# Fused block-sparse attention and gated projection on one Trainium2 core: where GpSimd makes a row tile's fourth low part, and where the gathers of the values stand

## The chip, the cores and the metric

The kernel runs on one core of one Trainium2 chip. The core has a matrix engine (TensorE, PE in the profile; PEld is its weight load), a vector engine (VectorE, DVE), a scalar engine (ScalarE, ACT), GpSimd (POOL), and SyncE (SP), which here only issues DMAs. Each engine works through its own instructions in order, and the engines wait for each other by semaphores. The metric is the device time of one execution in microseconds, as a median over several executions.

## The reference, cut to what matters

Attention over 4 batches, 8 heads, 768 positions and a head width of 64, in blocks of 32 positions. A query block sees itself, its two neighbours, the first and the last block, and three sampled blocks; the first and last query blocks see everything. Then a gated projection over d = 512:

```python
scores = where(mask, q @ k.T / 8, -1e9);  x = softmax(scores) @ v        # (B, S, 512)
gate   = sigmoid(sum_k conv_w[k] * shift(x, 4 - k))                      # causal, 5 taps, per channel
out    = (gate * (x @ w_val)) @ w_out
```

All of it is float32 in and out.

## The kernel before, in words

**Attention.** The work of a batch is 11 pairs of query blocks and one global pair (the first and last blocks), which counts as two units; 52 units in all. The main loop (lines 704 to 768) is a software pipeline over steps n. A step computes the scores of unit n on TensorE (`sc`, for global units `s`; `scores`, line 374), the transposes of unit n-1 (`pt`, line 423) and the values of unit n-2 (`av`, line 434). VectorE takes the maxima (`mx`), ScalarE the exponentials (`pe`) and the copies of the transposes out of PSUM (`ptr`). `finish` (line 476) turns the result around on TensorE (`xp`) and ScalarE copies it to `xT`. The scores of a global unit need a PSUM buffer in batches 2 and 3 that `xp` held, so TensorE waits there until ScalarE has made the copy `xT`.

**Keys and values.** GpSimd copies neighbour key blocks of a pair into `kg` two steps ahead (`copy_keys`, line 299). The rows of `v` that a pair needs are gathered by two indirect DMAs that GpSimd issues (`vb`, in `load_values`, line 317). `next_values` (line 742) issues them in step n for a pair that is read by the values of step n+3. The buffer that they fill is the one that the values of step n free, so each pair of gathers waits for the `av` matmuls of its own step.

**Projection.** 384 rows of a batch make a row tile; there are eight, numbered 1 to 8 here. Float32 operands are split into a high and a low part that TensorE multiplies in three passes. ScalarE makes the high parts (`xh`, `yh`), GpSimd the low ones (`xl`, `yl`) by a subtraction that needs the high part. VectorE builds the gates (`th`, a chain of multiply-adds with both tensor inputs in SBUF) and the product of gate and value projection (`y`, in `evict`).

`project` (line 551) is a generator, and each call of `advance` runs one piece of it. Pieces 1 to 4 are the value projections `vp` of the four column groups f = 0 to 3. Pieces 5 to 10 are the halves of three output groups `op`. In the kernel before, low part f is made by `second(f)`:

```python
for f in range(CH):            # piece f + 1
    if f > 1: second(f - 2)
    if f: evict(f - 1)
    ...                        # the 12 matmuls of vp[f], then yield
second(CH - 2)                 # piece 5: the third low part
evict(CH - 1)                  #          and the fourth y and yh
```

Piece 5 then issues the first half of the first `op`. Piece 6 begins with `second(CH - 1)`, the fourth low part, and then issues the second half of that `op`, whose last three matmuls are on group 3: twice its high part, and last its low part. `y` has two buffers, so `evict(f)` waits for `second(f - 2)`.

**The order around the change.** In each step the loop passes over the halves of `transposes`; in half i it calls `fill(FILLS[2n+i])`, which runs that many pieces of the projection, then `prepare`, which runs pieces of the gates (`th`) and of the split (`xh`, `xl`) of a later row tile, then `next_values`. `next_values` also stands ahead of the halves (line 746), and there it issues what is to be issued, unless `before_last_low` says that piece 6 falls into the first half of this step; then the gathers come behind that half. FILLS and STEPS are strings of digits written by hand.

By these strings piece 5 and piece 6 fall so: row tile 1, step 23 second half and step 24 first half; tile 2, step 29 second and step 30 first; tile 3, step 35 first and step 35 second; tile 4, step 40 second and step 41 first; tile 5, step 45 third pass (a global unit has three) and step 46 first; tile 6, step 51 second and step 52 first; tiles 7 and 8 behind the loop. Gathers are issued in steps 23, 24, 29, 30, 35, 40 and 41; in steps 45, 46, 51 and 52 none is left to issue. Step 29 begins with its scores at 172.2 us, step 30 at 179.0 us, step 35 at 215.9 us, and step 36 at 224.6 us.

Of the kernel before, what the change touches and what calls it, by code (L numbers as in the profile page):

```python
# [22 lines left out]
CH = 4  # L23
# [9 lines left out]
LAG_T, LAG_V = 1, 2  # L33
# [13 lines left out]
FILLS = (  # L47
    "11111210010222221221011022"
    "22111000222222111202211111"
    "02021011111110020111111002"  # L50
    "11211111221001111120020111"
    "1200"
)
# [11 lines left out]
def attention_moe(ctx, tc, qb, kb, v, ve, sampled, w_val, conv_w, w_out, ident_in, slot_in, out):  # L65
# [97 lines left out]
    def indices(b):  # L163

        row = const.tile([128, NB], F32, tag=f"row{b % 2}", name="row")
        dve.tensor_scalar_add(row, base, float(b * S - B * S))
        dve.tensor_tensor(out=row, in0=row, in1=valid, op=ALU.mult)
        dve.tensor_scalar_add(idx[:, b, :], row, float(B * S))
# [100 lines left out]
    def block_numbers(pr, eng):  # L269

        mine = [n for n in range(2 * NR) if COPIED[pr.bt.b].get(n, SP) == eng]
        if not mine:
            return
        first = NR * PAIRS[pr.p][0] + mine[0]
        _, regs = nc.values_load_multi_w_load_instructions(
            sm[0:1, first : first + len(mine)], engines=[eng], min_val=0, max_val=NB - 1,
            skip_runtime_bounds_check_because="block numbers are drawn from [0, 24)",
        )
        for n, reg in zip(mine, regs):
            yield 5 + 4 * (n // NR) + n % NR, reg  # L280
# [270 lines left out]
    def project(m):  # L551

        yh = const.tile([128, CH, TS], F32R, tag="yh", name="yh")
        yl = const.tile([128, CH, TS], F32R, tag="yl", name="yl")
        ys, vps = {}, {}

        def evict(f):
            y = ys[f] = two.tile([128, TS], F32, tag="y", name="y")[:, 0 : m.n]
            dve.scalar_tensor_tensor(
                out=y, in0=m.th[:, f, 0 : m.n], scalar=1.0, in1=vps[f][:, 0 : m.n], op0=ALU.add, op1=ALU.mult  # L560
            )
            act.copy(yh[:, f, 0 : m.n], y)

        def second(f):
            pool.tensor_tensor(
                out=yl[:, f, 0 : m.n], in0=ys[f], in1=yh[:, f, 0 : m.n].bitcast(F32), op=ALU.subtract
            )

        for f in range(CH):
            if f > 1:  # L570
                second(f - 2)
            if f:
                evict(f - 1)
            vps[f] = ps_moe.tile([128, 512], F32, tag="mo", name="vp")
            n = 0
            for wn, xn in ((0, m.xh), (1, m.xh), (0, m.xl)):
                for c in range(CH):
                    matmul(
                        vps[f][:, 0 : m.n], wv[wn][:, c, f * 128 : (f + 1) * 128], xn[:, c, 0 : m.n],
                        start=n == 0, stop=n == 11,  # L580
                    )
                    n += 1
            if f == CH - 1:
                unread.discard(id(m))
            yield
        second(CH - 2)
        evict(CH - 1)
        gating.discard(id(m))

        def leave(r, op):  # L590
            ot = two.tile([128, DM], F32, tag="ot", name="ot")
            row = m.t + r * 128
            if m.bt.b == B - 1 and row + 128 == S:
                act.activation(ot[:, 0:256], op[:, 0:256], AF.Copy, scale=0.5)
                dve.tensor_scalar(out=ot[:, 256:512], in0=op[:, 256:512], scalar1=0.5, scalar2=None, op0=ALU.mult)
                act.dma_start(out[m.bt.b, row : row + 128, 0:256], ot[:, 0:256])
                sp.dma_start(out[m.bt.b, row : row + 128, 256:512], ot[:, 256:512])
                return
            act.activation(ot, op, AF.Copy, scale=0.5)
            stores.append((out[m.bt.b, m.t + r * 128 : m.t + r * 128 + 128, :], ot))  # L600

        before = None
        for r in range(m.n // 128):
            op = ps_moe.tile([128, 512], F32, tag="mo", name="op")
            n = 0
            terms = [(f, yh, w) for f in range(CH - 1) for w in wo] + [(f, yl, wo[0]) for f in range(CH - 1)]
            for f, yn, w in terms + [(CH - 1, yh, wo[0]), (CH - 1, yh, wo[1]), (CH - 1, yl, wo[0])]:
                matmul(op, yn[:, f, r * 128 : (r + 1) * 128], w[:, f, :], start=n == 0, stop=n == 11)
                n += 1
                if n == 6:  # L610
                    if before is not None:
                        leave(*before)
                    yield
                    if r == 0:
                        second(CH - 1)
            before = r, op
            yield
        leave(*before)

    to_gate, to_split, to_project = [], [], []  # L620
    unread, gating, stores = set(), set(), []

    def store():
        while stores:
            sp.dma_start(*stores.pop(0))
# [27 lines left out]
    def may_project():  # L653
        return "all" in decoded and to_project and step[0] > max(to_project[0][0].ready)
# [4 lines left out]
                to_project[0][0].groups += 1  # L659
                advance(to_project)  # L660

    def before_last_low(times):

        return may_project() and to_project[0][0].groups <= CH + 1 < to_project[0][0].groups + times

    def prepare(steps):
        for _ in range(steps):
# [15 lines left out]
    def freed(k):  # L683

        return units[min(k, N - 1)].pr.seq if k >= 0 else -1

    def more(which, upto, load):
        if at[which] < len(pairs) and pairs[at[which]].seq <= upto:
            load(pairs[at[which]])
            at[which] += 1  # L690
            return True

    def until(which, n, do):
        while at[which] < min(len(pairs), pairs.index(units[min(n, N - 1)].pr) + 1):
            do(pairs[at[which]])
            at[which] += 1
# [7 lines left out]
    for n in range(N + LAG_V):  # L704
        step[0] = n

        def more_keys():
            return more("keys", freed(n - 1) + RING, load_keys)

        def more_values():  # L710
            return more("values", freed(n - LAG_V - 1) + VRING, load_values)

        if n == 0:
            more_keys()
            numbers_first = {eng: list(block_numbers(pairs[0], eng)) for eng in (POOL, ACT)}
            until("scaled", 0, scale)
            indices(0)
            until("copied", 0, copy_keys)
            more_keys()
            until("copied", 1, copy_keys)  # L720
            more_values()
        else:
            while more_keys() or more_values():
                more_values()
        until("scaled", n + (SCALE_AHEAD if n else 1), scale)
        store()
        k = len(staged)
        if k < 2 * CH and n >= WEIGHTS_AT[k] and (k < 4 or k - 4 in decoded):
            next(weights)

        if n < N:
            scores(units[n])
        if n == 0:
            more_keys()
        until("copied", n + COPY_AHEAD, copy_keys)
        if n == 0:
            while more_keys() or more_values():
                more_values()
        if 0 <= n - LAG_V < N:
            values(units[n - LAG_V])  # L740

        def next_values():
            while more("values", freed(n - LAG_V) + VRING, load_values):
                pass

        if n >= LAG_V and not before_last_low(int(FILLS[min(2 * n, len(FILLS) - 1)])):
            next_values()
        if 0 <= n - LAG_T < N:
            for half, _ in enumerate(transposes(units[n - LAG_T])):
                at_half = 2 * n + min(half, 1)  # L750
                fill(int(FILLS[at_half]))
                prepare(int(STEPS[at_half]))
                if n >= LAG_V:
                    next_values()
        else:
            fill(1)
            prepare(int(STEPS[2 * n]))
        if 0 <= n - LAG_V < N and units[n - LAG_V].last:
            pr = units[n - LAG_V].pr
            finish(pr)  # L760
            pr.bt.done.add(pr.p)
            for t, (r0, rn) in enumerate(TILES[pr.bt.b]):
                need = {p for p in range(NP - 1) if any(r0 <= i * BLK < r0 + rn for i in PAIRS[p])}
                if r0 == 0 or r0 + rn == S:
                    need.add(-1)
                if t not in pr.bt.queued and need <= pr.bt.done:
                    pr.bt.queued.add(t)
                    queue_rows(pr.bt, t)
# [53 lines left out]
```

## Time and profile before

| | |
|---|---|
| median of 3 runs | 384.92 us (383.56 to 385.92) |
| the profiled execution | 385.59 us, of which its span is 383.8 us |
| PE busy | 350.1 us (91%) |
| PEld busy | 275.0 us (72%) |
| DVE busy | 264.1 us (69%) |
| ACT busy | 253.6 us (66%) |
| POOL busy | 221.0 us (58%) |
| DMA | 72.37 MB, mean 189 GB/s |

Busy shares are means over the span; TensorE at 91% leaves 33.7 us of the span in which it has no matmul. In the rows, "[1.06 <-POOL yl L83]" means that the engine sat idle for 1.06 us before the row's first instruction, and that what ended the idle time was GpSimd's `yl`. All instructions pass through one helper, so every row says L83; operations are told apart by their tiles. "x4" is a run of four instructions that a view merges, and its duration is theirs together.

### The profile page before, as it was taken

To read this page: it belongs to the slowest core of one execution; us is meant where nothing else is said; L and a number is where in the kernel's file an instruction comes from. 1 tells how busy PE (TensorE), PEld (TensorE's weight loads), DVE (VectorE), ACT (ScalarE), POOL (GpSimd) and SP (SyncE) were. 2 spreads that over 40 slices of the span, in tenths; PEclk is the share of its full clock that TensorE was granted. 3 is DMA by queue.
4 is the path that set the end of the run, shared out by engine and by line. 5 is a ranking of instruction groups with operands and counts; after the bars stand their busy time and mean duration, and the time that the engine had idled before them with its cause. 6 is when DMAs were issued, how large, how long until landed. Compare 5 with 4: busy or idle time off the path is not lost.

```text
span 383.8 us, 15523 instructions
## 1 busy us (share of the span) xinstructions
PE 350.1 (91%) x6274; PEld 275.0 (72%) x6274; DVE 264.1 (69%) x546; ACT 253.6 (66%) x619; POOL 221.0 (58%) x309
## 2 busy tenths in 40 slices
PE   8788869878967999999899979999999999999895
PEld 7365556556646887788679857787787879789794
DVE  4346476866897779477978877656769877959520
ACT  1857697887788758765776756756666766565321
POOL 1885566897486486757553266556633753444640
PEclk9969999999999999999999989999999999999999
DMA  7997982999991546789786337788773373110102
GB/s 235 300 300 238 344 278 59 280 263 300 320 297 52 133 126 195 217 286 286 205 241 213 81 108 226 203 271 246 205 203 112 96 224 113 33 56 30 56 28 84
DMA packets 52584, 72.37 MB, mean 189 GB/s; under 512 B 6944, under 2 KB 34720, under 8 KB 52512
## 3 DMA queue, kind: packets, MB, share of 16 engines
q1 hardware_dynamic: 44896, 47.69, 40.7%
q0 software_dynamic: 7040, 23.43, 21.1%
q8 instruction: 50, 0.82, 0.9%
q10 hardware_dynamic: 576, 0.24, 0.2%
q14 instruction: 22, 0.18, 0.2%
HBM read 65.05 MB, written 6.29 MB: 186 GB/s over the span
## 4 chain that ended last, share of the span: by engine, by line
PE 65%; DVE 16%; ACT 7%; issue 6%; POOL 3%; DMA 1%; ACTq 1%; DVEq 0%
PE av L83 13%; PE op L83 13%; PE vp L83 13%; PE sc L83 11%; PE pt L83 9%; DVE th L83 7%; DVE mx L83 4%; PE xp L83 3%; PE s L83 3%; ACT pe L83 2%; ACT ptr L83 1%; DVE x L83 1%; POOL vb L83 1%; DMA sb<-in_sampled 1%; ACT kg L83 1%
## 5 line engine op out<-in xcount | busy, mean ns | idle before, releaser
L83 POOL DMA_INDIRECT vb<-in_v,idx x88 | 89.7, 1019 | 91.4 <-PE av L83 66.1
L83 DVE SCALAR_TENSOR_TENSOR th<-xT,cw,th 128x384 f32<-128x384 f32 x128 | 111.0, 875 | 11.8 <-ACT th L83 9.5
L83 ACT ACTIVATE pe<-sc,mx 128x256 f32<-128x256 f32 x176 | 69.0, 476 | 47.0 <-DVE mx L83 42.2
L83 DVE TENSOR_REDUCE mx<-sc 128x2 f32<-128x512 f32 x88 | 56.5, 683 | 47.9 <-PE sc L83 36.7
L83 ACT COPY ptr<-pt 128x512 f32<-128x512 f32 x112 | 64.9, 602 | 4.5 <-PE pt L83 4.0
L83 POOL TENSOR_TENSOR yl<-y,yh 128x384 fp32r<-128x384 f32 x32 | 34.7, 1091 | 38.6 <-ACT yh L83 38.2
L83 POOL COPY kg<-k 128x256 f32<-128x256 f32 (+1 forms) x143 | 52.2, 402 | 8.1 <-DMA k<-in_k 8.0
L83 PE MATMUL op<-wo,yh 128*128 128x512 f32 x192 | 53.7, 401 | 0.3 <-DVE y L83 0.3
L83 PE MATMUL sc<-kg,qc 64*32 64x256 f32 x1408 | 52.0, 392 | 2.1 <-issue 1.0
L83 PE MATMUL pt<-ident,pe 128*128 128x128 f32 x352 | 52.1, 283 | 0.4 <-issue 0.4
L83 PE MATMUL vp<-xh,wv 128*128 128x384 f32 x256 | 51.3, 341 | 0.0
L83 PEld LDWEIGHTS av<-va,ptr 128*32 128x32 f32 (+1 forms) x1056 | 31.7, 120 | 24.5 <-issue 14.9
L83 PE MATMUL av<-va,ptr 128*32 128x65 f32 (+1 forms) x1056 | 41.3, 229 | 4.5 <-ACT ptr L83 2.2
L83 PEld LDWEIGHTS pt<-ident,pe 128*128 128x128 f32 x352 | 39.6, 142 | 7.0 <-issue 0.9
L83 PEld LDWEIGHTS vp<-xh,wv 128*128 128x128 f32 x256 | 44.1, 188 | 0.2
L83 PE MATMUL av<-vb,ptr 128*32 128x65 f32 x1408 | 40.0, 225 | 2.6 <-issue 2.4
L83 PEld LDWEIGHTS op<-wo,yh 128*128 128x128 f32 x192 | 34.6, 188 | 7.5 <-DVE y L83 0.8
L83 POOL TENSOR_TENSOR xl<-xT,xh 128x384 fp32r<-128x384 f32 x32 | 35.4, 1111 | 6.1 <-ACT xh L83 5.9
L83 PEld LDWEIGHTS sc<-kg,qc 64*32 64x32 f32 x1408 | 23.3, 108 | 17.6 <-issue 9.8
L83 PE MATMUL op<-wo,yl 128*128 128x512 f32 x96 | 32.0, 413 | 3.3 <-POOL yl L83 3.3
L83 PEld LDWEIGHTS av<-vb,ptr 128*32 128x32 f32 x1408 | 31.1, 112 | 4.8 <-issue 3.2
L83 DVE SCALAR_TENSOR_TENSOR y<-th,vp 128x384 f32<-128x384 f32 x32 | 17.5, 548 | 23.2 <-PE vp L83 12.8
(72 smaller groups left out, 448.8 us busy)
## 6 DMA issues: line engine op xcount, KB each, us to landing
kg<-in_k SPq DMA_DIRECT2D x165, 64.0 KB
vn<-in_v SPq DMA_DIRECT2D x12, 520.0 KB
qc<-in_q SPq DMA_DIRECT2D x48, 128.0 KB
k<-in_k SPq DMA_DIRECT2D x12, 512.0 KB
out<-ot SPq DMA_DIRECT2D x23, 256.0 KB
va<-in_v SPq DMA_DIRECT2D x44, 130.0 KB
wst<-in_w_val SPq DMA_DIRECT2D x4, 512.0 KB
wst<-in_w_out SPq DMA_DIRECT2D x4, 512.0 KB
```

Of the source, the lines that this page charges most:

```text
L83: made = getattr(self.eng, name)(*args, **kwargs)
```

## The change

`second(CH - 1)` moves from the beginning of piece 6 to piece 5, right behind `evict(CH - 1)`: GpSimd's third and fourth low parts follow each other, and the fourth waits for the `yh` that ScalarE makes from that `evict`. `before_last_low` is replaced by `last_lows`, which looks at both halves of the step and returns the half in which piece 5 falls, or -1. `next_values` then stands ahead of the halves only for -1, and behind a half only from the returned one on.

```diff
@@ -585,6 +585,7 @@
             yield
         second(CH - 2)
         evict(CH - 1)
+        second(CH - 1)
         gating.discard(id(m))
 
         def leave(r, op):
@@ -611,8 +612,6 @@
                     if before is not None:
                         leave(*before)
                     yield
-                    if r == 0:
-                        second(CH - 1)
             before = r, op
             yield
         leave(*before)
@@ -659,9 +658,15 @@
                 to_project[0][0].groups += 1
                 advance(to_project)
 
-    def before_last_low(times):
-
-        return may_project() and to_project[0][0].groups <= CH + 1 < to_project[0][0].groups + times
+    def last_lows(fills):
+
+        if may_project():
+            groups = to_project[0][0].groups
+            for half, times in enumerate(fills):
+                if groups <= CH < groups + times:
+                    return half
+                groups += times
+        return -1
 
     def prepare(steps):
         for _ in range(steps):
@@ -743,14 +748,15 @@
             while more("values", freed(n - LAG_V) + VRING, load_values):
                 pass
 
-        if n >= LAG_V and not before_last_low(int(FILLS[min(2 * n, len(FILLS) - 1)])):
+        lows = last_lows([int(FILLS[i]) for i in (2 * n, 2 * n + 1) if i < len(FILLS)])
+        if n >= LAG_V and lows < 0:
             next_values()
         if 0 <= n - LAG_T < N:
             for half, _ in enumerate(transposes(units[n - LAG_T])):
                 at_half = 2 * n + min(half, 1)
                 fill(int(FILLS[at_half]))
                 prepare(int(STEPS[at_half]))
-                if n >= LAG_V:
+                if n >= LAG_V and min(half, 1) >= lows:
                     next_values()
         else:
             fill(1)
```

So the gathers of steps 23, 29 and 40 stand behind the second half, those of step 35 behind the first half, and those of steps 24, 30 and 41 ahead of the first half. In step 45 the third pass is not looked at and the function returns -1. GpSimd's order in step 29 was: two gathers, `yl` 1, `yl` 2, an `xl`; it becomes `yl` 1, `yl` 2, `yl` 3, an `xl`, two gathers (low parts counted from 0). In step 35 it was: two key copies, two gathers, `yl` 2, an `xl`, `yl` 3, an `xl`; it becomes two key copies, `yl` 2, `yl` 3, an `xl`, two gathers, an `xl`. Behind the loop, in tile 7, `yl` 3 passes one `xl`. The DMAs of `va` that SyncE issues are in `next_values` too; between the old and the new place SyncE has nothing else.

## Rows read from the trace of the kernel before

**Rows 1.** What TensorE's matmuls waited for from 126 us to the end: waiter, what ended the wait, total in us, times, longest.
```profile
PE op L83 <- POOL yl L83: 3.3, 3, 1.3
PE s L83 <- ACT xT L83: 1.9, 2, 1.7
PE pt L83 <- ACT ptr L83: 0.6, 2, 0.3
```

**Rows 2.** Busy time by engine in four stretches (start:end, length, busy us of each engine with its instructions, the granted TensorE clock as a share of full speed, DMA share, GB/s).
```profile
126.00:170.00 44.00, 44.00 (x716) 36.65 (x715) 31.69 (x68) 30.45 (x77) 27.33 (x35) 1.00 0.69 196
170.00:190.00 20.00, 18.31 (x375) 14.43 (x373) 17.11 (x29) 13.21 (x32) 13.26 (x16) 1.00 0.78 235
...
202.00:232.00 30.00, 28.00 (x459) 22.64 (x447) 22.62 (x39) 19.32 (x46) 14.48 (x18) 0.94 0.46 138
...
300.00:345.00 45.00, 44.60 (x789) 36.42 (x788) 34.82 (x62) 30.03 (x71) 22.53 (x25) 1.00 0.37 108
```

**Rows 3.** GpSimd's waits over the whole span, the longest group.
```profile
POOL vb L83 <- PE av L83: 66.1, 26, 6.6
```

**Rows 4.** GpSimd in order of time, steps 29 and 30 (row tile 2): start, duration, engine, operation, tiles, count, idle time before.
```profile
171.78 1.01 POOL L83 TENSOR_TENSOR yl<-y,yh 128x384 fp32r<-128x384 f32 x1
174.66 0.96 POOL L83 DMA_INDIRECT vb<-in_v,idx  x1 [1.87 <-PE av L83]
...
176.89 1.99 POOL L83 TENSOR_TENSOR yl<-y,yh 128x384 fp32r<-128x384 f32 x2
178.84 1.00 POOL L83 TENSOR_TENSOR xl<-xT,xh 128x384 fp32r<-128x384 f32 x1
179.80 1.00 POOL L83 TENSOR_TENSOR yl<-y,yh 128x384 fp32r<-128x384 f32 x1
```

**Rows 5.** ScalarE, VectorE and TensorE in order of time, from the same steps (the row of 165.00 is a `th` of step 28).
```profile
175.97 0.55 ACT L83 CAST yh<-y 128x384 fp32r<-128x384 f32 x1
...
178.53 0.51 ACT L83 CAST yh<-y 128x384 fp32r<-128x384 f32 x1 [0.38 <-DVE y L83]
...
187.42 0.42 ACT L83 COPY xT<-xp 128x256 f32<-128x256 f32 x1
...
165.00 0.61 DVE L83 SCALAR_TENSOR_TENSOR th<-xT,cw,th 128x384 f32<-128x384 f32 x1
...
178.41 3.77 DVE L83 SCALAR_TENSOR_TENSOR th<-xT,cw,th 128x384 f32<-128x384 f32 x1
182.10 1.27 DVE L83 TENSOR_REDUCE mx<-sc 128x2 f32<-128x512 f32 x2
...
187.89 0.67 PE L83 MATMUL s<-k,qc 64*32 64x256 f32 x16 [1.69 <-ACT xT L83]
```

**Rows 6.** GpSimd in order of time, step 35 (row tile 3).
```profile
218.35 0.99 POOL L83 DMA_INDIRECT vb<-in_v,idx  x1 [6.59 <-PE av L83]
...
220.90 1.00 POOL L83 TENSOR_TENSOR yl<-y,yh 128x384 fp32r<-128x384 f32 x1
221.84 1.01 POOL L83 TENSOR_TENSOR xl<-xT,xh 128x384 fp32r<-128x384 f32 x1
222.81 0.98 POOL L83 TENSOR_TENSOR yl<-y,yh 128x384 fp32r<-128x384 f32 x1
```

**Rows 7.** ScalarE and TensorE in order of time, step 35.
```profile
215.69 0.51 ACT L83 CAST yh<-y 128x384 fp32r<-128x384 f32 x1 [1.02 <-DVE y L83]
...
219.66 0.55 ACT L83 CAST yh<-y 128x384 fp32r<-128x384 f32 x1
...
221.95 0.50 PE L83 MATMUL op<-wo,yl 128*128 128x512 f32 x1 [1.06 <-POOL yl L83]
...
223.85 0.50 PE L83 MATMUL op<-wo,yl 128*128 128x512 f32 x1 [0.94 <-POOL yl L83]
```

**Rows 8.** Busy time by engine in the stretch behind these waits; the columns are those of rows 2.
```profile
224.20:226.50 2.30, 2.30 (x37) 0.81 (x35) 1.41 (x2) 1.19 (x3) 1.65 (x3) 0.53 0.32 92
```

**Rows 9.** The chain that ended last, in order of time (start, duration, what), in steps 36 and 37.
```profile
224.67 1.89 PE sc L83 x32
226.56 1.65 PE av L83 x64
...
232.24 1.02 PE sc L83 x32
233.26 1.07 PE av L83 x64
```

**Rows 10.** GpSimd, ScalarE and TensorE in order of time behind the loop (row tile 7).
```profile
354.47 1.35 POOL L83 TENSOR_TENSOR xl<-xT,xh 128x384 fp32r<-128x384 f32 x1
355.77 1.31 POOL L83 TENSOR_TENSOR yl<-y,yh 128x384 fp32r<-128x384 f32 x1
...
354.13 0.51 ACT L83 CAST yh<-y 128x384 fp32r<-128x384 f32 x1 [0.30 <-DVE y L83]
...
357.13 0.50 PE L83 MATMUL op<-wo,yl 128*128 128x512 f32 x1 [1.34 <-POOL yl L83]
```

**Rows 11.** How long a pair of gathers takes to land, and when one is read. First the first gather of a pair in GpSimd's order of time (the second follows at 285.57); then the DMA view of 290 to 304 us, the row of the queue that carries only the gathers (packets, MB, share of 16 engines); then TensorE in order of time in step 38, where the pair gathered in step 35 is read first.
```profile
284.30 0.97 POOL L83 DMA_INDIRECT vb<-in_v,idx  x1 [6.34 <-PE av L83]
...
q0 software_dynamic: 1, 0.00, 0.0%
...
238.18 0.31 PE L83 MATMUL av<-vb,ptr 128*32 128x65 f32 x8
```

## The prediction

> **What bounds the kernel now.** I began with the share of busy time: TensorE has matmuls in 91% of the span, no other engine in more than 69%. Whether that is a bound is seen by stretches. From 126 to 170 us TensorE is busy 44.00 of 44.00 us, from 300 to 345 us 44.60 of 45.00 [rows 2]: there nothing can be won by moving other engines' work. Holes are in 170 to 190 us (1.7 us) and in 202 to 232 us (2.0 us, at a granted clock of 0.94). So the next view is TensorE's own waits: the largest from 126 us on are 3.3 us for `yl`, in three places, and 1.9 us of the scores `s` for `xT` [rows 1]. Only these can turn into time. GpSimd's own long wait, 66.1 us of gathers for `av` [rows 3], costs nothing by itself; it matters where low parts queue behind it. Third, I read GpSimd in order of time around each row tile.
>
> **Step 35 (tile 3).** The reader sees a gather that waited 6.59 us for the values of its own step and began at 218.35, and behind it `yl` 2 only at 220.90, an `xl`, and `yl` 3 at 222.81 [rows 6]. TensorE waited 1.06 us for the first and 0.94 us for the second [rows 7]. With the change the gathers stand behind. `yl` 2 needs only its `yh`, cast from 215.69 for 0.51 us, so it can end at about 217.2. `yl` 3 needs the `yh` cast from 219.66 for 0.55 us; with 1.0 us of its own it ends at about 221.2. TensorE came to its first late matmul at 221.95 - 1.06 = 220.89 and has that one and two more before the one on `yl` 3, at 0.23 us each in an undisturbed run; so it gets there at about 221.5. Both waits go: **2.0 us**. If VectorE slows `yl` 3 to the 1.35 us of the slowest subtractions [rows 10], it ends at 221.6, and 0.1 us is left, which I neglect.
>
> **The clock behind it.** Right after these two waits the granted clock is 0.53 [rows 8], near the 1.2 GHz level, and the same 32 score matmuls take 1.89 us against 1.02 one step later, the same 64 value matmuls 1.65 against 1.07 [rows 9]: 0.87 + 0.58 = 1.45 us. No wait, no fall, as I read it; the bounds are 0 (the fall has another cause) and 1.45. In favour of 0: the 1.69 us wait at 186 us left the clock of its stretch at 1.00 [rows 2]. In favour of 1.45: it is the only fall in the second half and it stands directly behind the only two close waits. I take **1.45 us**.
>
> **Steps 29 to 31 (tile 2).** Here no matmul waits for `yl`; the cost goes round. The gathers began at 174.66, and `yl` 1, 2, an `xl`, `yl` 3 and an `xl` then ran without a gap from 176.89 to 180.8 [rows 4], the `xl` to some 181.8. A `th` of VectorE that began at 178.41 took 3.77 us where one like it takes 0.61, and ended when GpSimd's run did; the maxima of step 30 came behind it, at 182.10; ScalarE's order pushed the `xT` copy to 187.42, and the scores waited 1.69 us for it [rows 5]. With the change `yl` 1 follows `yl` 0 (done at 172.8), `yl` 2 follows its `yh` (175.97 + 0.55) and ends at 177.5, and the fourth `y` no longer waits for `yl` 1: its `vp` ends at about 177.0 and its `yh` some 0.5 us sooner than 178.53. `yl` 3 then runs at about 178.6, so there is a gap in GpSimd's work in which the `th` fits; the maxima start when their scores end, at 180.0, about 2 us sooner, and `xT` comes at about 185.7, before the first 32 score matmuls are through. The bounds are 0 and 1.69; I take **1.7 us**, because 2 us sooner is more than the wait.
>
> By the Trainium skill (GPSIMD Engine Reference, section Key points) GpSimd shares SBUF interfaces with VectorE and collides with VectorE instructions that have two SBUF inputs, as `th` has; the 3.77 us agree. By that rule alone a closer row of low parts speaks against the change, and it is the second rival below.
>
> **Tile 7, behind the loop.** `yl` 3 stands behind an `xl` of 1.35 us, and TensorE waits 1.34 us for it [rows 10]. Its `yh` is ready at 354.64; without the `xl` ahead it ends at about 354.64 + 1.31 = 355.95 instead of 357.08: **1.1 us**. The passed `xl` and its three followers end when they did, at 361 us, and the `vp` that reads them comes at 363, then at 362; so nothing is late next.
>
> **What costs nothing.** Tiles 1 and 4 lie in stretches where TensorE is full, the first in 126 to 170 us [rows 2]; earlier low parts bring nothing there. Tile 5 has no gathers near its low parts and tile 6 none left, and no matmul there waits for `yl`. Low part for low part GpSimd does the same work. The moved gathers: a pair begun at 284.30 has nothing but one packet left after 290 us [rows 11], so a pair takes under 6 us. The pair of step 35 starts at about 222.3 instead of 218.35 and lands by 228.3; it is read at 238.18 [rows 11], or some 5 us sooner by the gains before it, so 4 to 5 us of cover remain. Step 29's starts 6 us later, at about 180.7, and its reader is three steps off, at 195. Without that cover every us late is a us of TensorE. Behind the waiting `yl` 3 are queued the `xl`, the gathers and the key copies of the next step; the copies are made two steps ahead, and 1 to 4 us later is within one step of some 6 us. The gathers of steps 24, 30 and 41, now ahead of the halves, still come behind those of the step before, so they start about when they did, and the `xl` behind them about 1 us later, for a `vp` several steps on. On SyncE's queue the `va` loads pass nothing.
>
> **The sum.** 2.0 + 1.45 + 1.7 + 1.1 = 6.25 us; the other 0.2 us of `s` and the 0.6 us of `pt` I don't count. The profiled execution took 385.59 us, so 379.3; it stands 0.67 above the median of the runs, which would give 378.7. I say **379.0 us**.
>
> **Rivals.**
> *Half of it.* The scores of step 31 still wait, because ScalarE's row of casts and exponentials holds `xT` for its own reasons, or the clock falls anyway. One of them: 380.6 to 380.8; both: 382.2. For it: both gains are indirect, and of the two waits near 2 us only one was followed by a slower clock. Against it: the chain of waits runs through exactly these instructions.
>
> *VectorE is held off longer.* With `yl` 2, `yl` 3 and an `xl` back to back GpSimd runs some 3 us in one piece at five tiles in the loop. If a `th` is caught behind each, as in step 29, four tiles more pay what that one paid, 1.7 us: 6.8 us, and the tile that pays now goes on paying. Against them stand 2.0 + 1.1 + 1.45: a net 2.3 us slower, 387.2; if two of the new waits bring the clock down as at 224 us, another 2.9: 390. It decides at the point where `yh` 3 is ready before `yl` 2 has ended, so that no gap is left. Against it: `yh` 3 comes 2.6 and 4.0 us after `yh` 2 [rows 5, 7], and the gathers behind now break the run, where before the pieces ran some 4.9 us together [rows 4].
>
> *Gathers land late.* If GpSimd reaches the moved pair of a step more than 5 us later than I place it, the values three steps on wait. Four pairs at 2 us, and 1.45 us of clock with each, make 14 us less the 6.25 won: 392. Nothing in the waits of before hints at it.
>
> *It does not matter.* What TensorE wins is lost at the next thing that keeps pace with it: VectorE's chain, or the loads of keys, at a DMA share of 0.78 in 170 to 190 us [rows 2]. Then 383 to 385. Against it: from 126 to 170 us, at a DMA share of 0.69, TensorE ran 44 us without a wait, so the others kept up.
>
> **How the numbers follow.** About 1% is what a measurement of this kernel tells from no change; from 384.92 that is 381.1 and 388.8. Forecast, with its own range of 377 to 381: 0.50. Half of it: 0.22, half of that still beyond 1%. It does not matter: 0.17. VectorE held off: 0.06, mostly slower by more than 1%. Late gathers: 0.05, slower. So faster 0.59, same 0.34, slower 0.07. The range reaches from 376.8, the forecast with the 0.8 us not counted and 1.2 us for unlike executions, to 385.0, where half of it and no effect are inside.
>
> **What the profile after will show.** If right: in step 35 two low parts ahead of the gathers, no `op` waiting for `yl` there, and the granted clock at full in the step behind; in step 30 no `th` of over 1.5 us ahead of the maxima, and no wait of `s` for `xT` at the global unit; `op` waits for `yl` fall from 3.3 us to under 0.5. Wrong, if values wait for a `vb` load, if a `th` of 3 us or more stands ahead of the maxima in more steps than before, or if TensorE's waits only change their names.

## The result, and the profile after

The changed kernel took 387.85 us as a median of 21 runs (385.67 to 392.24); the kernel before, run beside it, took 385.89 us (382.75 to 389.80). The ratio is 1.0063, with an interval of 1.0043 to 1.0084: a little slower, where 379.0 us had been forecast. The medians here are over all runs, the ratios over the fast runs alone (a kernel has slower runs now and then), so the one is not quite the quotient of the others. The profiled execution took 389.33 us with a span of 387.5 us, 3.7 us more than before.

First TensorE's waits from 126 us on, in the changed kernel (waiter, what ended the wait, total in us, times, longest):

```profile
PE av L83 <- issue: 3.6, 8, 0.8
PE pt L83 <- ACT rest L83: 2.4, 1, 2.4
PE vp L83 <- ACT ot L83: 1.4, 1, 1.4
PE s L83 <- ACT xT L83: 1.1, 1, 1.1
```

The 3.3 us of `op` waiting for `yl` [rows 1] are gone altogether. Four other lines stand in their place, and the first has no releaser: TensorE's value matmuls `av` were held up, and no semaphore that the profile shows is to blame. Next the stretches (columns as in rows 2); the second and third are those of [rows 2] and [rows 8]:

```profile
190.00:202.00 12.00, 9.57 (x144) 7.28 (x142) 9.65 (x25) 6.04 (x13) 4.73 (x7) 0.86 0.75 220
202.00:232.00 30.00, 28.43 (x560) 23.24 (x559) 21.49 (x42) 20.26 (x48) 13.94 (x18) 1.00 0.50 143
224.20:226.50 2.30, 2.23 (x19) 1.41 (x24) 2.27 (x3) 1.79 (x6) 2.19 (x2) 1.00 0.20 64
```

The clock no longer falls at 224 us (0.53 before, now 1.00). It falls in a new place instead, 190 to 202 us, behind the two waits of 1.1 and 2.4 us (of `s` and `pt`) above. So the sum has to be made by steps. A step's time runs here from the start of its scores to the start of the next step's, in us; the last five columns are for the sections below.

| step | before | changed | changed, chip 2 | second places, chip 2 | before, chip 14 | changed, chip 14 | early low part alone, chip 9 |
|---|---|---|---|---|---|---|---|
| 25 | 6.26 | 7.33 | 7.48 | 6.26 | 6.26 | 6.26 | 7.04 |
| 31 | 8.48 | 12.14 | 10.73 | 7.17 | 8.48 | 6.69 | 6.58 |
| 35 | 8.75 | 6.45 | 6.45 | 6.78 | 8.66 | 6.44 | 7.72 |
| 36 | 7.57 | 8.31 | 8.42 | 6.12 | 7.68 | 6.13 | 6.11 |
| 42 | 6.11 | 7.24 | 7.28 | 6.11 | 6.11 | 6.11 | 6.11 |
| 43 | 9.75 | 11.05 | 9.37 | 9.76 | 9.76 | 9.33 | 9.76 |

Steps 25, 31, 36, 42 and 43 lost 1.07 + 3.66 + 0.74 + 1.13 + 1.30 = 7.90 us. Step 35 won 2.30 and the stretch behind the loop 1.26; 0.65 was won before step 24, where nothing was changed, so that is no effect of it. Together 3.7 us lost, the difference of the spans. Step 43's loss is one wait for an output tile's DMA (`vp` for `ot`, 1.4 us) that the later profiles of the changed kernel don't have; I leave it aside as a difference of executions.

**Where step 36 lost.** GpSimd, TensorE and VectorE of the changed kernel in order of time:

```profile
227.04 0.99 POOL L83 DMA_INDIRECT vb<-in_v,idx  x1
228.34 0.95 POOL L83 DMA_INDIRECT vb<-in_v,idx  x1 [0.30 <-issue]
...
226.31 1.09 PE L83 MATMUL sc<-kg,qc 64*32 64x256 f32 x32
227.33 0.33 PE L83 MATMUL av<-va,ptr 128*32 128x65 f32 x8
...
228.33 0.28 PE L83 MATMUL av<-va,ptr 128*32 128x65 f32 x3 [0.45 <-issue]
229.06 0.23 PE L83 MATMUL av<-va,ptr 128*32 128x65 f32 x1 [0.45 <-issue]
...
229.77 0.22 PE L83 MATMUL av<-vb,ptr 128*32 128x65 f32 x1 [0.40 <-issue]
...
230.60 0.66 PE L83 MATMUL pt<-ident,pe 128*128 128x128 f32 x4
...
229.84 1.29 DVE L83 TENSOR_REDUCE mx<-sc 128x2 f32<-128x512 f32 x2 [2.80 <-remote]
```

The 64 value matmuls run from 227.33 to the transposes at 230.60, 3.27 us, where 64 took 1.07 in step 37 before [rows 9]. There are three gaps beside the two gathers that GpSimd issues: the first lies across the end of the first gather, the second within the second, the third just behind it. The scores were through at 227.40, and yet the maxima that need nothing else from TensorE began at 229.84 ("remote" stands where the profile names no instruction of this core for the wait's end). So two things were late: TensorE's matmuls, and the news of finished ones.

**Where step 31 lost.** GpSimd, VectorE, ScalarE and TensorE of the changed kernel, steps 30 and 31:

```profile
181.42 0.97 POOL L83 DMA_INDIRECT vb<-in_v,idx  x1
182.69 0.94 POOL L83 DMA_INDIRECT vb<-in_v,idx  x1 [0.30 <-issue]
184.52 0.95 POOL L83 DMA_INDIRECT vb<-in_v,idx  x1 [0.88 <-PE pt L83]
185.77 0.95 POOL L83 DMA_INDIRECT vb<-in_v,idx  x1 [0.31 <-issue]
186.74 1.96 POOL L83 TENSOR_TENSOR xl<-xT,xh 128x384 fp32r<-128x384 f32 x2
...
184.28 0.16 DVE L83 TENSOR_SCALAR rs<-av 128x4 f32<-128x4 f32 x1 [2.38 <-PE pt L83]
...
185.04 5.09 DVE L83 SCALAR_TENSOR_TENSOR th<-xT,cw,th 128x384 f32<-128x384 f32 x4
...
190.25 1.01 DVE L83 TENSOR_REDUCE mx<-s 128x1 f32<-128x512 f32 x2
...
191.55 0.47 ACT L83 ACTIVATE rest<-s,mx 128x256 f32<-128x256 f32 x1 [3.58 <-DVE mx L83]
...
181.28 0.32 PE L83 MATMUL av<-vb,ptr 128*32 128x65 f32 x8
...
194.16 1.11 PE L83 MATMUL pt<-ident,pe 128*128 128x128 f32 x4 [2.43 <-ACT rest L83]
```

Here the matmuls themselves ran on (they are large ones), but the row sums `rs`, which need the `av` that ended at 181.60, began at 184.28, when both gathers of step 29's pair had been issued. The second pair, which had waited for the same `av`, got it late too, at 184.52. ScalarE waited 1.48 us for the transposes `pt`. From there it is a chain: four `th` begin 2.2 us later in their step than in the undisturbed run on chip 14, below, and run into GpSimd's two `xl`, where they take 5.09 us; the maxima of the global unit follow at 190.25, `rest` at 191.55 and its second half at 193.63, and TensorE waits 2.43 us. By the Trainium skill (GPSIMD Engine Reference, section Key points) these two engines collide where VectorE has two SBUF inputs; the trace agrees, with 5.09 us against 2.57 us for the same four `th` in the early low part alone, below. The transposes behind the wait then run at the slower clock of the stretch of 0.86. That clock is a part of the loss, an estimated 1.4 us: on chip 2, below, the same two waits left the granted clock of 190 to 202 us at 1.00, and step 31 took 10.73 us in place of 12.14.

**The same in the kernel before.** It had this once from 126 us on. GpSimd and TensorE of the kernel before, in order of time, step 39:

```profile
241.40 1.13 POOL L83 DMA_INDIRECT vb<-in_v,idx  x1 [3.59 <-issue]
242.84 0.98 POOL L83 DMA_INDIRECT vb<-in_v,idx  x1 [0.30 <-issue]
...
243.46 0.29 PE L83 MATMUL av<-vb,ptr 128*32 128x65 f32 x3 [0.26 <-issue]
244.16 0.22 PE L83 MATMUL av<-vb,ptr 128*32 128x65 f32 x1 [0.42 <-issue]
```

Over the whole span of the kernel before, the first 126 us included, TensorE's waits have:

```profile
PE av L83 <- issue: 4.6, 9, 1.0
```

These gaps were in reach, and the prediction did not read them. The kernel's rule of place can be read from GpSimd's 66.1 us of waiting [rows 3]: before, a gather mostly waits for the `av` of its own step, and so is issued when TensorE's small matmuls of that step are over.

### The profile page after: what moved, and what is told of

Its sections match the earlier page's. It is cut to its first block, busy times and chain, and to the rows that moved or that the text cites. A ratio compares the mean times of both kernels' runs of the same rounds, so it can differ in the third digit from the quotient of the medians.

```text
span 387.5 us, 15526 instructions
## 1 busy us (share of the span) xinstructions
PE 352.0 (91%) x6274; PEld 275.9 (71%) x6274; DVE 259.1 (67%) x546; ACT 254.1 (66%) x619; POOL 220.9 (57%) x309
## 4 chain that ended last, share of the span: by engine, by line
PE 61%; DVE 18%; issue 6%; DMA 5%; ACT 5%; SPq 2%; POOL 1%; ACTq 1%; POOLq 0%; DVEq 0%
PE op L83 13%; PE av L83 12%; PE vp L83 11%; PE sc L83 10%; PE pt L83 10%; DVE th L83 8%; DVE mx L83 6%; PE xp L83 3%; DMA kg<-in_k 2%; DMA k<-in_k 2%; PE s L83 2%; ACT pe L83 1%; SPq L83 1%; POOL yl L83 1%; DVE x L83 1%
## 5 line engine op out<-in xcount | busy, mean ns | idle before, releaser
L83 POOL DMA_INDIRECT vb<-in_v,idx x88 | 88.8, 1009 | 73.5 <-PE av L83 48.8
L83 DVE SCALAR_TENSOR_TENSOR th<-xT,cw,th 128x384 f32<-128x384 f32 x128 | 105.9, 835 | 13.1 <-ACT th L83 10.8
L83 PE MATMUL pt<-ident,pe 128*128 128x128 f32 x352 | 52.9, 285 | 2.7 <-ACT rest L83 2.4
L83 PE MATMUL op<-wo,yh 128*128 128x512 f32 x192 | 54.7, 408 | 0.3 <-DVE y L83 0.2
L83 PE MATMUL sc<-kg,qc 64*32 64x256 f32 x1408 | 50.9, 384 | 2.3 <-POOL kg L83 1.3
L83 PEld LDWEIGHTS av<-va,ptr 128*32 128x32 f32 (+1 forms) x1056 | 32.5, 118 | 27.6 <-issue 18.9
L83 PE MATMUL av<-va,ptr 128*32 128x65 f32 (+1 forms) x1056 | 42.8, 226 | 7.2 <-issue 4.9
L83 PEld LDWEIGHTS op<-wo,yh 128*128 128x128 f32 x192 | 35.4, 193 | 7.8 <-DVE y L83 0.8
```

Of the source, the lines that this page charges most:

```text
L83: made = getattr(self.eng, name)(*args, **kwargs)
```

## The experiments

The theory after the result: **while GpSimd issues a pair of gathers, and shortly behind, TensorE's small score and value matmuls are held up, and its reports to other engines come late; the change moved pairs into such places.** Rivals: the early low part, packed against the third, holds VectorE off (the prediction's second rival); or the order of GpSimd's own work, its low parts and splits, is worse. The runs were made on four chips, with the kernel before beside them each time; on chips 14, 0, 2 and 9 it took 379.0, 381.3, 387.4 and 384.9 us.

**Each half of the change alone, and the whole again (chip 14).** The low part alone, on the kernel before:

```diff
         second(CH - 2)
         evict(CH - 1)
+        second(CH - 1)
...
-                    if r == 0:
-                        second(CH - 1)
```

> The fourth low part moves to piece 5 as in the change; the gathers keep their places of before. Theory G (gathers that GpSimd issues while TensorE works through the scores and values of a step hold TensorE back, and the change moved them there): no gather is moved, so nothing is lost; tile 7 gains its 1.1 to 1.3 us and step 35 about 0.9 us, 0.993 to 0.999 of before. Theory L (packed low parts hold VectorE off its multiply-adds): the loss is in here, 1.004 to 1.010 of before.

The gathers alone: `last_lows` and the two places of `next_values` as in the change, the low part left in piece 6.

> The gathers move as in the change; the fourth low part stays in piece 6. Theory G: the loss of the change without its gains, 1.006 to 1.015 of before, with score-and-value stretches of over 3 us in some of steps 24, 36 and 41 where others take 2.1 us; in step 35 the fourth low part now comes behind the gathers, and the output matmul waits 3 us or more for it. Theory L: 0.995 to 1.001.

The changed kernel and the kernel before, both without an edit, the second for its profile:

> The change once more, unaltered, for a second profile. Theory G: the same stretches as in the first profile, at steps 24, 36 and 41 (value matmuls of one step 2 to 3.1 us instead of 1.1) and the late reports of TensorE in step 30, since they go with the places of the gathers; 1.004 to 1.009 of before. If they were accidents of one execution, they stand elsewhere or are gone.

> The kernel before once more, for a second profile. Theory G: the value matmuls of steps 24, 36 and 41 take 1.1 us again; the two waits of step 35 and the slower clock behind them come again. If the clock's fall at 224 us was an accident, it is gone while the waits remain.

Measured: the low part alone 378.0 us, ratio 0.9989 (0.9946 to 1.0032); the gathers alone 388.81 us, 1.0283 (1.0231 to 1.0334); both, 372.76 us, **0.9872 (0.9820 to 0.9924)**. So on this chip the change is faster, nearly as the prediction had it. The theory had put 1.004 to 1.009 here, with slow value matmuls at three steps; neither came. (The steps that the expectations call 24 and 41 are 25 and 42 in the table.) The gathers alone are slow for a plain reason, in TensorE's waits of that kernel:

```profile
PE op L83 <- POOL yl L83: 9.4, 5, 3.0
```

The fourth low part then stands behind the moved gathers and comes late. Of the changed kernel on this chip, TensorE's largest waits from 126 us on:

```profile
PE pt L83 <- ACT ptr L83: 0.6, 2, 0.4
PE op L83 <- DVE y L83: 0.3, 2, 0.2
```

And GpSimd and TensorE there in order of time, step 36:

```profile
214.30 0.99 POOL L83 DMA_INDIRECT vb<-in_v,idx  x1
215.59 0.95 POOL L83 DMA_INDIRECT vb<-in_v,idx  x1 [0.30 <-issue]
...
213.56 1.09 PE L83 MATMUL sc<-kg,qc 64*32 64x256 f32 x32
...
215.66 0.66 PE L83 MATMUL pt<-ident,pe 128*128 128x128 f32 x4
```

Pair and values stand side by side as in the result's trace (the pair 0.74 us behind the start of the scores, there 0.73), and the step has no gap: 2.10 us from the scores to the transposes, there 4.29. So the place of the gathers does no harm by itself; it does it on some chips. The profiles of before agree in the waits that the prediction went by: 3.3 us for `yl` and 1.9 for `xT` are there on chip 14 as in [rows 1]. They differ in another: the `av` gaps without a releaser, 4.6 us in 9 places, are all gone on chip 14. So the two kinds of chip show in the profile of the kernel before already. The low part alone stood at no difference, but its profile has one 3.1 us wait of `vp` for `ot` in step 43, as the result's had one of 1.4, so its number is taken again below.

**Again on another chip, and other places for the gathers (chip 0).** The second kernel is the changed one with its low parts, but with the gathers ahead of the halves, as before, in every step but two: in step 29 they come behind the first half, in step 35 between the third low part and the fourth.

> The change once more, unaltered. In the runs so far it is 1.0063 of before with a before of 385.9 us, and 0.987 with a before of 379.0 us. Theory G': whether gathers hold TensorE back belongs to the chip or its session; if TensorE's reports stand still at nearly each pair of gathers in the profile, this comes to 1.002 to 1.009, if they hardly do, to 0.983 to 0.992. A rival, that the two results are chance on one kind of chip, gives something in between with no such tie.

```diff
         evict(CH - 1)
+        if between[0]:
+            between[0]()
         second(CH - 1)
...
-        lows = last_lows([int(FILLS[i]) for i in (2 * n, 2 * n + 1) if i < len(FILLS)])
+        between[0] = next_values if n == 35 else None
+        lows = {29: 0, 35: 0}.get(n, -1)
```

> The fourth low part early as in the change; gathers ahead of the halves in every step but 29 (behind the first half) and 35 (between the third and the fourth low part), so each pair begins right behind the values of its own step. Theory G': no pair runs beside scores and values more than before, so the gains stay on either kind of chip: 0.982 to 0.991. Theory L (packed low parts hold VectorE off): no better than the change.

Measured: the changed kernel 373.13 us, **0.9840 (0.9781 to 0.9898)**; the second places 377.0 us, 0.9886 (0.9832 to 0.9940). Both faster; on such a chip the second places bring nothing more.

**Extra gathers (chip 0).** To see the hold-up by itself, the kernel before got fourteen more pairs, of key rows into a tile that nobody reads, in steps 33 to 48: in one kernel issued beside scores and values (behind a small copy of `xT`), in the other behind the step's own gathers (behind a copy of `x`).

```diff
+        if 33 <= n <= 48 and not pr.glob:
+            for j, i in enumerate(PAIRS[pr.p]):
+                pool.indirect_dma_start(out=spare[:, j, :], out_offset=None, in_=kb.rearrange("p b n x -> (p b n) x"),
+                    in_offset=bass.IndirectOffsetOnAxis(ap=idx[:, pr.bt.b, i : i + 1], axis=0))
```

> The kernel before with 14 extra pairs of gathers of 512 bytes a row (into a tile that nothing reads) in steps 33 to 48, begun when the copy xT ends a step, so beside the scores and values of the next. Theory G' on a chip that holds TensorE back: the score and value stretches of these steps grow from 2.1 to 3 us and more, 10 to 30 us in all; on one that does not: under 5 us. If GpSimd's own time is what costs, it is as slow as the extra pairs behind the values.

> The same extra pairs, but behind each step's own gathers and behind the x of its values. Theory G': the same GpSimd work and the same bytes as beside the scores and values, yet 0 to 8 us on either kind of chip, and less than there by most of the loss.

Measured: beside, 387.12 us, 1.0201 (1.0123 to 1.0278); behind, 396.33 us, 1.0428 (1.0347 to 1.0508). The order is the wrong way round for the theory, and the profile of the first has no gap of `av` at all: steps 36 to 38 took 6.13, 4.74 and 4.78 us. What both lost here, 5.8 and 15.0 us where I had written under 5 and 0 to 8, was GpSimd's own time ahead of its low parts, in TensorE's waits for `yl` (4.1 and 8.9 us) and for `y` (5.2 and 7.2 us). On this chip, then, the theory's mechanism is not there, and the pair of kernels says nothing of it.

**On a chip that behaves like the first (chip 2).** The changed kernel and the second places once more:

> The change once more, unaltered, to meet the first kind of session. Theory G': where the kernel before takes about 386 us and the profile shows TensorE's reports standing still at most pairs of gathers, this is 1.002 to 1.009 of before; where before takes 378 to 381 us and the reports come on time, 0.983 to 0.990.

> The low parts of the change with each pair of gathers right behind the values of its own step (steps 29 and 35 as before in this study). Theory G': in a session of the first kind the loss of the change is gone, 0.985 to 0.995; in one of the second kind 0.983 to 0.992, as measured.

Measured: the changed kernel 388.62 us, **1.0109 (1.0021 to 1.0196)**, slower again; the second places 380.56 us, **0.9880 (0.9833 to 0.9926)**. TensorE's waits in the changed kernel on this chip:

```profile
PE av L83 <- issue: 3.6, 9, 0.5
PE pt L83 <- ACT rest L83: 2.4, 1, 2.4
PE s L83 <- ACT xT L83: 1.3, 1, 1.3
```

And VectorE's row sums of step 30 in it, in the view in order of time:

```profile
185.05 0.16 DVE L83 TENSOR_SCALAR rs<-av 128x4 f32<-128x4 f32 x1 [2.42 <-PE pt L83]
```

The same lines as in the first profile, within 0.2 us, at the same steps (the table): not an accident of one execution. Only the clock did not fall this time. TensorE's waits with the second places:

```profile
PE av L83 <- issue: 0.8, 2, 0.4
PE pt L83 <- issue: 0.8, 2, 0.4
PE op L83 <- POOL yl L83: 0.4, 1, 0.4
```

And in order of time GpSimd in steps 30 and 35 and the same row sums of VectorE:

```profile
181.37 0.96 POOL L83 DMA_INDIRECT vb<-in_v,idx  x1 [0.66 <-PE av L83]
...
217.22 0.99 POOL L83 DMA_INDIRECT vb<-in_v,idx  x1 [1.06 <-PE av L83]
...
219.77 1.02 POOL L83 TENSOR_TENSOR yl<-y,yh 128x384 fp32r<-128x384 f32 x1
...
181.26 0.15 DVE L83 TENSOR_SCALAR rs<-av 128x4 f32<-128x4 f32 x1
```

The pairs wait for the `av` of their own step again, `rs` of step 30 has no wait, and steps 25, 31, 36 and 42 lose nothing. The low parts are as packed as in the change, the four `th` of step 30 even take 4.68 us, and it wins all the same: 8.06 us between two kernels that differ only in where the gathers stand (and with them SyncE's `va` loads). That decides against packed low parts. It changes GpSimd's order too, so against the second rival stands something else: on chips 14 and 0 the changed kernel has the very same order and wins.

**The hold-up by itself, and the low part alone (chip 9).** The extra pairs beside scores and values once more, and the early low part alone:

> The kernel before with fourteen more pairs of gathers, each issued when GpSimd has seen the copy xT, beside the scores and values of steps 33 to 48. Theory (a gather being issued holds TensorE's small matmuls back): on a chip where the changed kernel loses, TensorE's values av show issue gaps at the extra pairs, over 4 us in more than 10 places where the kernel before has 0.7 us in 2, and steps 36 to 38 take 7 to 8 us in place of 6.1, 4.7 and 4.8. On a chip where the changed kernel wins there are under 3 such gaps again, as in the earlier run. Rival (the losses of the changed kernel came from something else than gathers beside these matmuls, the order of GpSimd's work alone): under 3 such gaps on either kind of chip, with late low parts and y again as the only losses.

> The early fourth low part alone, the gathers where they were. Theory: on a chip where the changed kernel loses, this one does not lose, ratio 0.980 to 1.003, with at most 1.0 us of issue gaps at the values and no late row sums in step 30. Rival (the packed low parts themselves hold VectorE off on such a chip): a ratio over 1.005 there.

Measured: with the extra pairs 416.71 us in one run (before, 384.91). TensorE's largest wait from 126 us on:

```profile
PE av L83 <- issue: 15.6, 36, 1.1
```

And GpSimd and TensorE in order of time, step 37:

```profile
235.03 0.99 POOL L83 DMA_INDIRECT spare<-in_k,idx  x1 [0.35 <-issue]
236.33 0.94 POOL L83 DMA_INDIRECT spare<-in_k,idx  x1 [0.30 <-issue]
...
236.36 0.27 PE L83 MATMUL av<-vb,ptr 128*32 128x65 f32 x3 [0.42 <-issue]
237.09 0.22 PE L83 MATMUL av<-vb,ptr 128*32 128x65 f32 x1 [0.46 <-issue]
...
237.83 0.27 PE L83 MATMUL av<-vb,ptr 128*32 128x65 f32 x2 [0.40 <-issue]
```

36 gaps in place of 2; 33 of them follow the start of a gather that nobody reads, 3 that of one of `vb`. Steps 36 to 38 took 9.36, 7.20 and 7.35 us (the first more than I had written). The same kernel on chip 0 had no such gap. So gathers beside these matmuls make the gaps, without any `va` load moved, and only on some chips. The low part alone took 381.4 us here, **0.9909 (0.9870 to 0.9947)**: no loss. VectorE's four `th` behind the row sums of step 30 in it, where GpSimd makes no `xl` beside them:

```profile
184.79 2.57 DVE L83 SCALAR_TENSOR_TENSOR th<-xT,cw,th 128x384 f32<-128x384 f32 x4
```

Its `av` gaps were 1.2 us in 3 places, 0.2 more than expected, and its step 25 lost 0.78 us to one of them: there, too, the early low part had moved the pair of step 24 to 149.12, beside the scores of step 25, which start at 149.82. That chip 9 is of the first chip's kind rests on these gaps; the changed kernel itself was not run there.

## Why the prediction was wrong

**The gains were right, term by term.** Chip 14 shows them undisturbed, since before and changed ran there side by side. Step 35: 2.0 us forecast, 8.66 - 6.44 = 2.22 measured. The clock behind it: 1.45 forecast, 7.68 - 6.13 = 1.55. Step 31: 1.7 forecast, 8.48 - 6.69 = 1.79. Behind the loop: 1.1 forecast, 1.27. The sum was 6.25 us; from the start of step 31 to the end the two traces differ by 6.8. The forecast ratio, 379.3 over 385.59 or 0.984, lies in the intervals of chips 14 and 0.

Three of these arrived in the result's trace too: no `op` waits for `yl`, the clock at 224 us is 1.00 (rival "half of it" had doubted that), and tile 7's last low-part matmul comes without a wait. But step 31's 1.7 turned into a loss of 3.66, and step 36, though its clock stayed up, lost 0.74.

**The step that failed** is the one headed "What costs nothing", where it says of the moved gathers that "a pair takes under 6 us", that "4 to 5 us of cover remain", and that those of steps 24, 30 and 41 "start about when they did". It priced a gather by when its data land. The place of step 35's pair came out about right: it was forecast at 222.3 and began 0.7 us later, reckoned from its step's start (227.04, where the step began 4.0 us later than before). But 222.3 is beside the scores and values of step 36, and what else runs there was never asked. The pairs of steps 24, 30 and 41 did not "start about when they did": reckoned in the same way they began 2.1, 2.2 and 1.0 us later than before, and the second gathers of 24 and 41 so came beside the scores and values of steps 25 and 42. On the chip of the result this cost 7.9 - 1.3 = 6.6 us in steps 25, 31, 36 and 42, more than the gains that were left, and the forecast 1.7 and 1.45 at two of those steps were lost in it.

**The rivals.** VectorE held off by packed low parts, whose 387.2 us the result came nearest, is not what happened: the second places have the same low parts and gain 1.2% on the chip where the change loses. A `th` did run long in front of maxima, 5.09 us for four, but because the late `rs` had pushed it beside GpSimd's `xl`. No value waited for a `vb` load, so "gathers land late" is out. "It does not matter" has the result's kind of outcome by another road: the waits did not merely change names, new ones were made. By the prediction's own 1% the result is no change, to which it gave 0.34, but the road was an engine disturbed by another one's issue, which none of its rivals held. Three small slips in its sums alter nothing: counted from 379.0 one half lost is 380.5 to 380.7 us and not 380.6 to 380.8, and the foot of the range 377.0 and not 376.8, and its chances for faster add up to 0.61 and not 0.59.

**What stays open.** What makes the difference between chips. Chips 2 and 9 held TensorE back, as the chip of the result did, and chips 14 and 0 did not; but each ran in one session only, so it could also be the session. Nothing in the profile names what the matmuls waited for.

## What to carry to other kernels

When an instruction is moved, look at what the other engines do at the time of its new place, not only at its own queue and at when its data are read; on chips like 2 and 9 a gather issued by GpSimd is better put where TensorE runs large matmuls and where no engine waits for a report of it, here behind the values of its own step. Waits "<-issue" of small matmuls are worth a look even when they are 0.7 us in all: ask what ran beside them. And a change of about 1% is worth timing on more than one chip: here its sign differed, 0.984 on one and 1.011 on another, while the second places gained 1.1 to 1.2% on both chips where they ran.

## What the runs showed of the hardware

- On the chip of the result and on chips 2 and 9, a pair of gathers beside small matmuls leaves up to three gaps in TensorE's `av`, most of 0.3 to 0.5 us, whose ends lie some 0.73 us apart (228.33, 229.06, 229.77 in the changed kernel; 236.36, 237.09, 237.83 with the extra pairs): 1.3, 2.0 to 2.1 and 2.7 to 2.8 us after the pair began, the last just behind the second gather. By the Trainium skill (Perfetto Trace Analysis, section DMA Instruction — SWDGE (GPSIMD)) the profiled time of such an instruction ends when GpSimd has written the descriptors, not when the data have moved. Of the 3.6 us of gaps in the changed kernel 1.4 lie within that time, and the rest between the two gathers or just behind the second; so they begin with the writing and outlast it.
- Reports of TensorE to VectorE and to GpSimd's queue come late at the same time, also where TensorE's own matmuls ran without a gap: `rs` 2.7 us behind the end of its `av` in step 30, where the same kernel on chip 14 has 0.5.
- This differs from chip to chip, or from session to session, since each chip had one: the same extra pairs made 36 gaps on chip 9 and none on chip 0 from 126 us on.
